# The opening of a recurrent attention kernel laid out anew: first alphas turned by quarters, unread padding left uncleared, first scores and masks chunk by chunk, the second block's k and q turned in halves

## The chip, the cores and the metric

The kernel runs on one core of one Trainium2 chip. The metric is the device time of one execution in microseconds (us), lower is better. The core has five engines that each work through an instruction list of their own: TensorE (PE, matrix multiplications, into PSUM banks), VectorE (DVE), ScalarE (ACT), GpSimd (POOL) and SyncE (SP, which here only issues DMA transfers). Engines wait for each other through semaphores.

## The reference

Two steps, one after the other, for 4 batches, 8 heads, 768 time steps, head size 48:

```python
state = zeros((B, H, D, D))
for t in range(S):                                    # gated linear attention
    state = alpha[:, :, t, :, None] * state + einsum('bhd,bhe->bhde', k[:, :, t], v[:, :, t])
    y[:, :, t] = einsum('bhd,bhde->bhe', q[:, :, t], state)
x = y.transpose(0, 2, 1, 3).reshape(B, S, H * D)      # 384 columns
val, gate = split(x @ w_in)                           # w_in 384 x 1024, halves of 512
h = exp(A_log) * h + val[:, t, :]                     # scan over t, gives ys
out = (gate * sigmoid(gate) * ys) @ w_out             # w_out 512 x 384
```

w_in and w_out arrive as 64-bit floats, of which the kernel makes 32-bit ones on the chip.

## The kernel before, in words

The work is cut into 12 blocks: 4 batches of 3 blocks of 256 steps each (N=12, NG=3, GC=256). A block has two chunks of 128 steps (c = 0, 1), a chunk two halves of 64 steps. Heads 0 to 3 lie on partitions 0 to 63 of a block's tensors and heads 4 to 7 on partitions 64 to 127; i = 0, 1 names the two groups of heads.

For each block m:

- alpha, q and k come from memory with steps on partitions (`load_steps`) in the first blocks, and are *turned* on TensorE so that head and head dimension lie on partitions: `turned` (L684) writes into a PSUM bank, `copy_turned` (L698) copies the bank into place, `turn_over`, `alphas` and `straighten` (L705 to L721) do both. A block's tensor has eight pieces j, two banks of four. For most tensors a piece is turned by two matmuls with the identity, one for each group i, each into one half of the array's columns (L694, two trace records each); for the four listed in `turned` it is a transpose of 128 columns and one of 64 (L689, L690, one record each).
- VectorE scans alpha's running product P (`scan_P`, L630) and the reverse one V (`scan_V`, L649), and multiplies Zk = k V (`scaled_k`, L614) and Zq = q P (`scaled_q`, L605).
- TensorE makes `scores` (L744), 32 trace records for each chunk; `masks` has VectorE cut the scores (L754) and ScalarE copy the K and dS parts out (L756).
- TensorE then makes the output y of values inside the block (`first_values` L862 for block 0, `values` L778 later), the block's state sums (`states`, L810), and the part carried from state sums (`first_carried` L870, `carried` L791). For block 0 `first_states` puts the sums into wide_S (ScalarE L877, VectorE L879).
- `first_join` (L884 to L887) or `join` copies y as xT, and `project(n, cc)` (L927) multiplies it by a quarter of w_in; ScalarE makes sg (L940), VectorE scans h (L932), and `output` multiplies by w_out (L956).

The weights come in six units. Each unit is converted in `convert(i)`: ScalarE makes the low part (`low`, L544, into a tile wr), VectorE two instructions of high bits (L553, L555), GpSimd adds both (L557).

Every list is written out by hand, each engine keeps the order in which the program issues its instructions, and the kernel uses eight PSUM banks: s0, s1, y0, y1 by name, and a ring of four called mm that `bank()` hands out in turn; a writer waits until the last reader of the bank's former content is done.

The opening (L982 to L1025) is a straight list. The first loads are issued on SyncE and ScalarE. The padding of several tiles is cleared by VectorE memsets (L497 to L516). After `convert(0)` a memset of one element of raw_a on GpSimd (L1001) holds back the second stream of loads: SyncE's next issue overwrites that tile, and everything SyncE issues later (alpha 2, w_in units 2 and 3, k 2, q 2, alpha 3, v 1, w_out, v 2) stands behind it. The first `project` closes the opening; block 1's scores, the turning of block 2's alpha, k and q, and project(0,1) to project(0,2) follow in the first pass of the loop:

```python
V = scan_V(1, P)
f0 = project(n, 0)
scaled_k(1, tk, V); scaled_q(1, tq, P); low(2)
f1 = project(n, 1)
convert(2); alphas(2); low(3)
first(m)                       # scores(1), masks(1)
f0(); f1()
tk = straighten(2, "k"); ...; tq = straighten(2, "q")
...
f2 = project(n, 2)
```

Of the kernel before, what the change touches and what calls it, by code (L numbers as in the profile page):

```python
# [11 lines left out]
U32 = mybir.dt.uint32  # L12
U16 = mybir.dt.uint16
AF = mybir.ActivationFunctionType
ALU = mybir.AluOpType
# [331 lines left out]
def fast(  # L347
# [27 lines left out]
    G = 2  # L375
# [117 lines left out]
    def constants():  # L493
# [18 lines left out]
        for t in dS[0] + dS[1]:  # L512
            nc.vector.memset(t[:, :, :, D:64], 0.0)
        for t in sums:
            nc.vector.memset(t[:, :, D:64], 0.0)
        nc.vector.memset(K0[:, :, :, D:], 0.0)  # L516
# [21 lines left out]

    def low(i):
        bits, w = bits_of(i)  # L540
        r = p2.tile([C, UW], I32, tag="wr", name="wr")
        lows[i] = r.rearrange("p (a n) -> p a n", a=w.shape[1])
        halves = lows[i].bitcast(U16).rearrange("p a (n two) -> p a n two", two=2)
        nc.scalar.activation(halves[:, :, :, 0], bits[:, :, :, 0], AF.Copy, scale=2.0 ** -29)  # L544

    def convert(i):
        if i not in lows:
            low(i)
        bits, w = bits_of(i)
        r = lows.pop(i)  # L550
        halves = r.bitcast(U16).rearrange("p a (n two) -> p a n two", two=2)
        quarters = bits.rearrange("p a n two -> p a (n two)").bitcast(U16).rearrange("p a (n four) -> p a n four", four=4)
        nc.vector.tensor_scalar(out=w.bitcast(U32), in0=bits[:, :, :, 1], scalar1=3, scalar2=0x3FFFFFFF,  # L553
                                op0=ALU.logical_shift_left, op1=ALU.bitwise_and)
        nc.vector.tensor_scalar(out=halves[:, :, :, 1], in0=quarters[:, :, :, 3], scalar1=0xC000, scalar2=None,  # L555
                                op0=ALU.bitwise_and)
        nc.gpsimd.tensor_tensor(out=w.bitcast(I32), in0=w.bitcast(I32), in1=r, op=ALU.add)  # L557
# [33 lines left out]
    def by_runs(t):  # L591
        return t.rearrange("p h (c j) -> p h c j", j=NJ)
# [90 lines left out]

    def turned(m, name, js, t):  # L684
        raw = steps_of(name, m)
        tp = t[:, 0:len(js) * C].rearrange("p (j x) -> p j x", j=len(js))
        if (m, name) in ((1, "k"), (1, "q"), (2, "a"), (3, "a")):
            for n, j in enumerate(js):
                nc.tensor.transpose(tp[:, n], raw[:, ds(ROW + j * D - 64, C)], ident)  # L689
                nc.tensor.transpose(tp[0:64, n], raw[:, ds(j * D, 64)], ident)  # L690
            return tp.rearrange("p j (c h) -> p h c j", h=4)
        for n, j in enumerate(js):
            for i in range(2):
                nc.tensor.matmul(tp[ds(64 * i, 64), n], raw[:, ds(i * ROW + j * D, 64)], ident,  # L694
                                 start=True, stop=True, skip_group_check=True)
        return tp.rearrange("p j (c h) -> p h c j", h=4)

    def copy_turned(to, js, tp, engine=None):  # L698
        place = by_runs(to)[:, :, :, js.start:js.stop]
        if engine:  # L700
            return engine.tensor_copy(out=place, in_=tp)
        return nc.scalar.activation(place, tp, AF.Copy)  # L702

    def turn_over(m, name, to, tags=(None, None)):
        size = NJ // len(tags)  # L705
        copies = []
        for n, tag in enumerate(tags):
            js = range(size * n, size * (n + 1))
            copy = copy_turned(to, js, turned(m, name, js, bank(tag)), nc.vector if n % 2 and tag else None)
            if tag:  # L710
                for other in copies[(n + 1) % 2::2]:
# [3 lines left out]
    def alphas(m, tags=(None, None)):  # L715
        turn_over(m, "a", by_place(als[m % 2])[:, :, 1:GP], tags)
# [31 lines left out]
    def masks(m):  # L748
        sc = [[t[:, 0:4 * (L + D)].rearrange("p (h x) -> p h x", h=4) for t in pair] for pair in scs.pop(m)]
        mb = mask[:, None, :]  # L750
        if m < NG:
            for c in range(G):
# [269 lines left out]
    first_carried((2, 3))  # L1022
    first_join()
    nc.scalar.activation(a_dec, a_log, AF.Exp)
# [196 lines left out]
```

## Time and profile before

| | us |
|---|---|
| median of 3 runs | 279.24 (279.05 to 279.8) |
| profiled execution | 279.67 |
| its span in the trace | 277.8 |
| busy: TensorE / VectorE / ScalarE / GpSimd | 271.7 / 217.8 / 110.3 / 98.2 |
| start of the first projection | 23.49 |
| SyncE's second stream of loads begins | 19.06 |

A span is the time from the first to the last instruction of the profiled execution. Rows of the chain of work that ended last give start, length, engine, output and line. Rows of an engine's timeline give start, busy time, line, operation, output<-input, shapes and count, and in brackets the idle time before with what ended it. A windows row gives, for a stretch of time, the busy time of TensorE, of its weight loads, VectorE, ScalarE and GpSimd, then the granted TensorE clock, the DMA engines' share and GB/s. "record" means one instruction of TensorE in the trace.

### The profile page before, as it was taken

The page shows a single profiled execution, that of the slowest core. Times are in us where ns is not written, and L with a number is a line of the kernel's source. Part 1 is how long each engine was busy: PE and PEld are TensorE (multiplying, and loading weights), DVE is VectorE, ACT ScalarE, POOL GpSimd, SP SyncE. Part 2 cuts the span into 40 slices and gives each one's busy share as a digit, 9 for nine tenths or more (in the row PEclk, how much of TensorE's full clock was granted, in tenths as well). Part 3 has the DMA queues.
Part 4 walks back from the last instruction along what each step waited for, and adds up shares of the span by engine and source line. Part 5 has one row for each costly group of instructions (what it writes and reads, how often), then busy time and mean ns, then how long its engine had stood idle before and what let it go on. Part 6 is the DMA issues. An engine that isn't in the chain of part 4 may idle for free.

```text
span 277.8 us, 9491 instructions
## 1 busy us (share of the span) xinstructions
PE 271.7 (98%) x4040; PEld 217.3 (78%) x4040; DVE 217.8 (78%) x281; ACT 110.3 (40%) x244; POOL 98.2 (35%) x105
## 2 busy tenths in 40 slices
PE   7999999999999999999999999999999999999995
PEld 5988987876688788788787787787787787787874
DVE  7889998898499599499499599499499598269640
ACT  2677763461325325325334334334343343341111
POOL 8131223230057155156156164164165163142000
PEclk9999999999999999999999999999999999999999
DMA  6949991935909739729659748829748711101101
GB/s 189 314 133 319 285 293 49 217 78 132 273 12 228 168 97 217 168 85 221 145 140 205 158 132 197 188 91 197 170 125 186 190 55 45 58 5 43 57 5 59
DMA packets 52462, 41.16 MB, mean 148 GB/s; under 512 B 27360, under 2 KB 50976, under 8 KB 52416
## 3 DMA queue, kind: packets, MB, share of 16 engines
q1 hardware_dynamic: 50768, 38.98, 55.3%
q10 hardware_dynamic: 1392, 0.99, 1.3%
q8 instruction: 32, 0.52, 0.8%
q0 software_dynamic: 256, 0.56, 0.7%
q14 instruction: 14, 0.11, 0.1%
HBM read 32.54 MB, written 4.72 MB: 134 GB/s over the span
## 4 chain that ended last, share of the span: by engine, by line
PE 94%; DVE 3%; DMA 1%; ACT 1%; issue 1%; SPq 0%; DVEq 0%; ACTq 0%
PE mm L927 47%; PE mm L956 20%; PE y L778 4%; PE y L791 4%; PE s L744 4%; PE mm L744 3%; PE s L810 3%; PE mm L1182 2%; DMA raw_a<-in_alpha_dram 1%; PE mm L694 1%; PE mm L689 1%; PE mm L690 1%; DVE V L649 1%; DVE P L630 1%; PE y L862 1%; PE s L694 1%
## 5 line engine op out<-in xcount | busy, mean ns | idle before, releaser
L927 PE MATMUL mm<-xT,w_in 128*128 128x256 f32 x576 | 133.4, 385 | 0.6 <-ACT xT L884 0.6
L927 PEld LDWEIGHTS mm<-xT,w_in 128*128 128x128 f32 x576 | 106.7, 190 | 17.1 <-issue 0.8
L956 PE MATMUL mm<-w_out,f_last 128*128 128x384 f32 x160 | 53.2, 486 | 0.0
L940 ACT ACTIVATE sg<-mm 128x256 f32<-128x256 f32 x48 | 18.4, 384 | 72.4 <-PE mm L927 71.9
L956 PEld LDWEIGHTS mm<-w_out,f_last 128*128 128x128 f32 x160 | 30.4, 190 | 19.1
L942 POOL TENSOR_TENSOR f_last<-sg,hh 128x256 f32<-128x256 f32 x36 | 34.3, 954 | 24.7 <-ACT sg L940 21.2
L830 POOL TENSOR_TENSOR sum<-sum,dS 128x192 f32<-128x192 f32 x30 | 31.2, 1039 | 18.2 <-ACT dS L818 16.8
L762 POOL TENSOR_TENSOR AK<-AK,mask 128x512 f32<-128x512 f32 x9 | 11.5, 1281 | 67.4 <-ACT AK L760 67.4
L649 DVE TENSOR_TENSOR_SCAN V<-al,ends 128x1028 f32<-128x1028 f32 x12 | 30.1, 2512 | 0.4
L932 DVE TENSOR_TENSOR_SCAN hh<-a_dec,hh,mm 128x256 f32<-128x256 f32 x32 | 23.1, 722 | 8.3 <-PE mm L927 8.1
L950 ACT ACTIVATE o_sb<-mm 128x384 f32<-128x384 f32 x22 | 10.8, 491 | 46.4 <-PE mm L956 46.4
L630 DVE TENSOR_TENSOR_SCAN P<-al,lower 128x1028 f32<-128x1028 f32 x12 | 27.5, 2292 | 0.4
L759 DVE TENSOR_TENSOR A<-s,mask 128x256 f32<-128x256 f32 x9 | 3.8, 425 | 29.5 <-PE s L744 29.5
L595 DVE STREAM_TRANSPOSE k<-raw_k 128x1024 f32<-128x1024 f32 x9 | 18.3, 2033 | 0.0
L595 DVE STREAM_TRANSPOSE q<-raw_q 128x1024 f32<-128x1024 f32 x9 | 18.1, 2016 | 0.0
L557 POOL TENSOR_TENSOR w_in<-w_in,wr 128x768 int32<-128x768 int32 x4 | 7.3, 1832 | 26.4 <-ACT al L702 9.5
L595 DVE STREAM_TRANSPOSE al<-raw_a 128x1024 f32<-128x1024 f32 x8 | 16.4, 2048 | 0.1
L605 DVE TENSOR_TENSOR Zq<-q,P 128x1024 f32<-128x1024 f32 (+1 forms) x14 | 15.0, 1070 | 0.3
L778 PEld LDWEIGHTS y<-AK,v 64*64 64x64 f32 x352 | 12.1, 134 | 3.6 <-issue 3.6
L614 DVE TENSOR_TENSOR Zk<-k,V 128x1024 f32<-128x1024 f32 (+1 forms) x14 | 14.7, 1050 | 0.1
L778 PE MATMUL y<-AK,v 64*64 64x64 f32 x352 | 14.5, 221 | 0.0
L778 PE MATMUL y<-A,v 64*64 64x64 f32 x352 | 14.5, 221 | 0.0
(158 smaller groups left out, 375.1 us busy)
## 6 DMA issues: line engine op xcount, KB each, us to landing
v<-in_v_dram SPq DMA_DIRECT2D x22, 192.0 KB, 4.0
out_dram<-o_sb SPq DMA_DIRECT2D x22, 192.0 KB, 4.2
raw_k<-in_k_dram SPq DMA_DIRECT2D x18, 184.0 KB, 3.6
raw_q<-in_q_dram SPq DMA_DIRECT2D x18, 184.0 KB, 4.2
raw_k<-in_k_dram SPq DMA_DIRECT2D x18, 176.0 KB, 4.1
raw_q<-in_q_dram SPq DMA_DIRECT2D x18, 176.0 KB, 4.3
raw_a<-in_alpha_dram SPq DMA_DIRECT2D x16, 184.0 KB, 5.2
raw_a<-in_alpha_dram SPq DMA_DIRECT2D x16, 176.0 KB, 5.1
```

The costliest lines, as they stand in the source:

```text
L595: nc.vector.transpose(out=by_runs(to).rearrange("p h c j -> p h j c"), in_=raws[name][:, 0:4 * ROW].rearrange("p (h j d) -> p h j d", h=4, ...
L605: nc.vector.tensor_mul(Zqs[m % 2][:, ds(u0, n), :, D:].rearrange("p u h t -> p h u t"), t[:, :, at].rearrange("p h (u t) -> p h u t", t=L) ...
L630: nc.vector.tensor_tensor_scan(out=P, data0=al[:, 0:4 * GP], data1=lower.rearrange("p h t -> p (h t)"), initial=0.0, op0=ALU.mult, op1=ALU ...
L649: nc.vector.tensor_tensor_scan(out=V[:, ::-1], data0=al[:, 1:4 * GP + 1][:, ::-1], data1=ends.rearrange("p h t -> p (h t)")[:, ::-1], init ...
L744: nc.tensor.matmul(scs[m][c][i][ds(L * h, L), ds(p * (L + D), L + D)], Zk[rows, c, p, ds(h * L, L)], Zq[rows, u, p], start=True, stop=True ...
L778: nc.tensor.matmul(ys[m][i][ds(64 * s, 64), e, ds(c * C + h * L, L)], v_sb[rows, c, 4 * i + p, :], As[i][rows, c, p, :], start=across and ...
L830: nc.gpsimd.tensor_add(Ss[j][:, :, 0:D], Ss[j - 1][:, :, 0:D], part)
L927: nc.tensor.matmul((pv, pg)[vg], w_ins[cc][:, kk, vg, :], xT[:, kk, :], start=(kk == 0), stop=(kk == NK - 1))
L932: nc.vector.tensor_tensor_scan(out=hh, data0=a_dec[:, cc:cc + 1].to_broadcast([C, GC]), data1=pv, initial=prev_h[cc][:, GC - 1:GC] if n % ...
L940: nc.scalar.activation(sg, pg, AF.Silu)
L942: f = lambda: engine.tensor_mul(fs[n][cc], sg, hh)
L956: nc.tensor.matmul(os[c], fs[n][cc][:, ds(c * C, C)], w_outs[cc // 2][:, cc % 2, :], start=(cc == 0), stop=(cc == NI - 1))
```

## The change

Only the opening is edited; from `for half in range(2): load_w_out` on the program is as before.

- **Padding.** The memsets of dS, K0 (columns that no instruction reads) are dropped; those of `sums` move to GpSimd, behind the second weight conversion.
- **First alphas.** `first_alphas` turns block 0's alphas by 32 matmuls of 64x64 (a quarter of the array each) where there were 16 of 128x64, beginning with the group i = 1 of the first two pieces. The four copies, two on ScalarE and two on VectorE, each take 16 step-places of four pieces.
- **First q, k.** `first_q` turns all eight pieces of group i = 1 first and then all of i = 0, where the groups alternated. Block 0's k is turned by transposes.
- **Weights.** `convert` is cut into `room`, `low`, `high` (which can take every other row group) and `add_low`. `convert(0)` stands after the masks of block 0 and block 1's second k copy; the high bits of unit 1 are made in two parts; `low(1)` and `add_low(1)` come after `first_states`.
- **Scores, masks, second block.** Scores of block 0 are issued by chunk, masks by chunk. Block 1's k is turned in two halves, one ahead of the scores and one behind them, and its q in two halves, one behind the states and one behind the carried parts, before `first_join`.
- **Small copies.** ratio and lower are copied between the scans.

The diff without its plainest lines:

```diff
@@ constants
         for t in vs:
             nc.vector.memset(t[:, :, :, D:64], 0.0)
-        for t in dS[0] + dS[1]:
-            nc.vector.memset(t[:, :, :, D:64], 0.0)
-        for t in sums:
-            nc.vector.memset(t[:, :, D:64], 0.0)
-        nc.vector.memset(K0[:, :, :, D:], 0.0)
@@ conversion
     def low(i):
+        nc.scalar.activation(room(i)[1][:, :, :, 0], bits_of(i)[0][:, :, :, 0], AF.Copy, scale=2.0 ** -29)
+
+    def high(i, part=slice(None)):
         bits, w = bits_of(i)
...
+        nc.vector.tensor_scalar(out=w.bitcast(U32)[:, part], in0=bits[:, part, :, 1], scalar1=3, scalar2=0x3FFFFFFF,
+                                op0=ALU.logical_shift_left, op1=ALU.bitwise_and)
+        nc.vector.tensor_scalar(out=halves[:, :, :, 1], in0=quarters[:, part, :, 3], scalar1=0xC000, scalar2=None,
+                                op0=ALU.bitwise_and)
+
+    def add_low(i):
+        w = bits_of(i)[1]
+        nc.gpsimd.tensor_tensor(out=w.bitcast(I32), in0=w.bitcast(I32), in1=lows.pop(i), op=ALU.add)
...
@@ turning
+    turned_by_transpose = ((0, "k"), (1, "a"), (1, "k"), (1, "q"), (2, "a"), (3, "a"))
...
-        if (m, name) in ((1, "k"), (1, "q"), (2, "a"), (3, "a")):
+        if (m, name) in turned_by_transpose:
...
+    def first_alphas():
+        raw, to = steps_of("a", 0), by_runs(by_place(als[0])[:, :, 1:GP])
+        tps = [[bank(tag)[:, 0:NJ // 2 * 64].rearrange("p (j x) -> p j x", x=64) for tag in tags]
+               for tags in (("s0", "s1"), ("y1", "y0"))]
+
+        def turn_quarter(j, i, r):
+            rows = ds(64 * r, 64)
+            nc.tensor.matmul(tps[j // 4][r][ds(64 * i, 64), j % 4], raw[rows, ds(i * ROW + j * D, 64)],
+                             ident[rows, rows], start=True, stop=True, skip_group_check=True)
+
+        for j in range(2):
+            for r in range(2):
+                turn_quarter(j, 1, r)
+        for j in range(NJ):
+            for r in range(2):
+                turn_quarter(j, 0, r)
+                if j + 2 < NJ:
+                    turn_quarter(j + 2, 1, 1 - r)
         copies = []
...
+                copy = nc.vector.tensor_copy(out=place, in_=part) if r else \
+                    nc.scalar.activation(place, part, AF.Copy)
...
+    def first_q():
+        raw, to = steps_of("q", 0), plain("q")
+        tps = [bank().rearrange("p (j x) -> p j x", x=C) for _ in range(2)]
+        for i in (1, 0):
+            for j in range(NJ):
+                nc.tensor.matmul(tps[j // 4][ds(64 * i, 64), j % 4], raw[:, ds(i * ROW + j * D, 64)], ident,
+                                 start=True, stop=True, skip_group_check=True)
...
@@ the opening's list
-    alphas(0, ("s0", "s1", "y1", "y0"))
-    tq = straighten(0, "q")
+    first_alphas()
+    tq = first_q()
     tk = straighten(0, "k")
     alphas(1)
     P = scan_P(0)
+    last = P[:, :, GC]
+    nc.scalar.activation(ratio[:, 0], last, AF.Copy, scale=1.0 / FIRST_PRODUCT)
+    nc.scalar.activation(lower[:, :, 0], last, AF.Copy)
     V = scan_V(0, P, False)
-    halves = [range(0, NJ // 2), range(NJ // 2, NJ)]
-    parts = [turned(1, "k", js, bank()) for js in halves]
+    part = turned(1, "k", halves[0], bank())
     for c in range(G):
         scaled_k(0, tk, V, c)
         scaled_q(0, tq, P, c)
-    scores(0)
     tk = plain("k")
-    for js, part in zip(halves, parts):
-        copy_turned(tk, js, part)
+    copy_turned(tk, halves[0], part)
+    for c in range(G):
+        scores(0, (c,))
+    part = turned(1, "k", halves[1], bank())
+    for c in range(G):
+        masks(0, (c,))
+    copy_turned(tk, halves[1], part)
+    high(0)
+    high(1, slice(0, None, 2))
     low(0)
-    parts = [turned(1, "q", js, bank()) for js in halves]
-    convert(0)
+    add_low(0)
     nc.gpsimd.memset(raws["a"][0:1, 0:1], 0.0)
     load_steps("a", 2, [nc.sync])
     load_w(units[2], nc.sync)
-    masks(0)
-    low(1)
     first_values(True)
     st = states(0)
-    convert(1)
+    tq = plain("q")
+    part = turned(1, "q", halves[0], bank())
     first_states(st)
-    tq = plain("q")
-    for js, part in zip(halves, parts):
-        copy_turned(tq, js, part)
-    last = P[:, :, GC]
-    nc.scalar.activation(ratio[:, 0], last, AF.Copy, scale=1.0 / FIRST_PRODUCT)
-    nc.scalar.activation(lower[:, :, 0], last, AF.Copy)
+    low(1)
+    copy_turned(tq, halves[0], part)
+    high(1, slice(1, None, 2))
+    add_low(1)
+    for t in sums:
+        nc.gpsimd.memset(t[:, :, D:64], 0.0)
...
     first_carried((1,))
     first_values(False)
     first_carried((2, 3))
+    part = turned(1, "q", halves[1], bank())
     first_join()
+    copy_turned(tq, halves[1], part)
```

More of the change, by code (lines that the diff above doesn't have):

```diff
@@ L537, in fast, with room @@
     lows = {}
+    def room(i):
+        if i not in lows:
+            r = p2.tile([C, UW], I32, tag="wr", name="wr")
+            lows[i] = r.rearrange("p (a n) -> p a n", a=bits_of(i)[1].shape[1])
+        return lows[i], lows[i].bitcast(U16).rearrange("p a (n two) -> p a n two", two=2)
     def low(i):
+        nc.scalar.activation(room(i)[1][:, :, :, 0], bits_of(i)[0][:, :, :, 0], AF.Copy, scale=2.0 ** -29)
+    def high(i, part=slice(None)):
         bits, w = bits_of(i)
[L541 to L544, printed above, removed]
+        halves = room(i)[1][:, part]
+        quarters = bits.rearrange("p a n two -> p a (n two)").bitcast(U16).rearrange("p a (n four) -> p a n four", four=4)
+        nc.vector.tensor_scalar(out=w.bitcast(U32)[:, part], in0=bits[:, part, :, 1], scalar1=3, scalar2=0x3FFFFFFF,
[5 more added lines that the diff above has]
+        nc.gpsimd.tensor_tensor(out=w.bitcast(I32), in0=w.bitcast(I32), in1=lows.pop(i), op=ALU.add)
     def convert(i):
@@ L548, in convert @@
             low(i)
[L549 to L557, printed above, removed]
+        high(i)
+        add_low(i)
     def check_w(i):
@@ L696, in turned @@
         return tp.rearrange("p j (c h) -> p h c j", h=4)
[L698 to L705, printed above, removed]
-        copies = []
[L707 to L711, printed above, removed]
+    halves = [range(0, NJ // 2), range(NJ // 2, NJ)]
@@ new lines, in copy_turned @@
+    def copy_turned(to, js, tp):
+        nc.scalar.activation(by_runs(to)[:, :, :, js.start:js.stop], tp, AF.Copy)
+    def first_alphas():
[14 more added lines that the diff above has]
+                    turn_quarter(j + 2, 1, 1 - r)
+        copies = []
+        for n in range(2):
+            for r in range(2):
+                place = to[:, :, ds(16 * r, 16), 4 * n:4 * n + 4]
+                part = tps[n][r].rearrange("p j (c h) -> p h c j", h=4)
+                copy = nc.vector.tensor_copy(out=place, in_=part) if r else \
+                    nc.scalar.activation(place, part, AF.Copy)
+                for other in copies[1 - r::2]:
@@ L718, in straighten, with turn_over, alphas @@
+    def turn_over(m, name, to):
+        for js in halves:
+            copy_turned(to, js, turned(m, name, js, bank()))
+    def alphas(m):
+        turn_over(m, "a", by_place(als[m % 2])[:, :, 1:GP])
     def straighten(m, name):
```

11 lines of the change are left out of this document (6 added, 5 removed).

## The prediction

> **What bounds the kernel now.** I read four views in turn: the page's parts 1 and 4, the chain of waits for the first 70 us, TensorE's own waits, then the timelines of the other engines up to 40 us. The page first:
>
> ```profile
> span 277.8 us, 9491 instructions
> PE 94%; DVE 3%; DMA 1%; ACT 1%; issue 1%; SPq 0%; DVEq 0%; ACTq 0%
> ```
>
> The chain that ended last is TensorE for 94% of the span, so a change pays only where it shifts TensorE's last instruction. The profiled execution took 279.67 us, 1.87 us more than its span and 0.43 us more than the 279.24 us median; I work in its microseconds and add the difference to the median.
>
> ```profile
> 4.72 1.80 PE s L694 x16
> 6.52 0.91 PE y L694 x16
> ...
> 10.59 2.31 DVE V L649
> ...
> 12.99 0.69 DVE Zk L614
> ...
> 18.53 0.90 PE y L862 x40
> ...
> 20.00 0.34 ACT wide_S L877
> ...
> 20.38 0.62 PE y L870 x22
> ...
> 22.98 0.37 ACT xT L884
> ...
> 23.49 5.42 PE mm L927 x24
> ...
> 31.58 0.77 PE mm L744 x32
> 32.35 3.64 PE mm L694 x64
> 35.99 2.79 PE mm L927 x12
> 39.40 0.72 PE s L810 x64
> PE mm L927 <- ACT xT L884: 0.6, 1, 0.6
> ```
>
> The chain's columns are start, length and work. Up to 15 us it runs over VectorE's scans P and V, then over TensorE; from the first projection (23.49) on it is TensorE almost alone, and the list of TensorE's waits between 15 and 70 us (last row) has little but the 0.6 us ahead of that projection. The change ends at that projection. So two questions decide: when it starts (23.49 now), and whether what the change delays holds up the stretch behind it, up to project(0,2) at 35.99.
>
> **The change up to the first projection.** Step by step along TensorE.
>
> First alphas. The first 16 records took 1.80 us and the next 16, of one shape, 0.91: TensorE ran at half rate until about 6.4. After, 32 quarter matmuls of 64x64 do the work, two records each, on four tiles. The nearest row is L810: 64 records of 48 columns on four tiles in 0.72, which for 64 columns gives 0.72 x 64/48 = 0.96, and at half rate 1.9. From 4.72, with a few records ahead of it because the half that arrives first goes first: an end at 6.4 (6.2 to 6.7) instead of 7.43, **1.0 us gained**. The copies are now two for each engine; those of the last bank run behind 6.4 and take 0.46 (VectorE's rows; the last is TensorE's first):
>
> ```profile
> 5.28 0.58 DVE L513 MEMSET dS<- 128x128 f32 x4
> ...
> 6.28 0.17 DVE L516 MEMSET K<- 128x128 f32 x1
> 6.56 0.46 DVE L701 COPY al<-s 128x256 f32<-128x256 f32 x1
> 1.44 2.93 PE L726 MATMUL y<-wide_S 128*128 128x256 f32 x6 [1.44 <-DVE raw_q L498]
> ```
>
> VectorE clears padding from 5.28 to 6.45 (L513 to L516: 11 memsets, the first four and the last shown) and copies at 6.56; the removal is what lets that copy run at 5.9. The six of L515 go to GpSimd at about 25, where it is idle. Behind them both scans move up 0.9: V from 10.59 to 9.7, ending at 12.0, and P ahead of it to 7.1.
>
> ```profile
> 7.21 1.93 PE L694 MATMUL mm<-ident,raw_q 128*64 128x128 f32 x32
> 8.96 1.93 PE L694 MATMUL mm<-ident,raw_k 128*64 128x128 f32 x32
> ...
> 12.56 0.33 PE L689 MATMUL mm<-ident,raw_k 128*128 128x128 f32 x1
> ...
> 14.26 0.27 PE L690 MATMUL mm<-ident,raw_k 128*64 128x128 f32 x1
> 14.46 1.00 PE L744 MATMUL s<-Zq,Zk 48*64 48x112 f32 x32
> 15.64 1.00 PE L744 MATMUL mm<-Zq,Zk 48*64 48x112 f32 x32 [0.18 <-ACT k L702]
> 10.95 0.60 ACT L702 ACTIVATE k<-mm 128x512 f32<-128x512 f32 x1 [0.30 <-PE mm L694]
> ```
>
> First q. Now two column halves alternate, 32 records start within 1.75 us (7.21 to 8.96), 0.055 each. After, eight matmuls on one half come first, then eight on the other. Bounds: 1.75 if TensorE overlaps them anyway, 3.5 if the 32 records queue singly at the 0.11 of two transposes (16 records from 12.56 to 14.37). L862 speaks for queueing: a record of its 64 columns is half of 0.11, 0.055; 40 spread evenly over four tiles would take 0.55; its order puts two thirds on one column half, whose two tiles then set 0.73; measured 0.90. I take 3.1, as the two halves overlap where they meet: **1.35 lost** (0 to 1.75). It ends at 9.6.
>
> k(0) by transposes: 16 records of 0.11, 1.75 as now, free; 11.35. a(1) then ends at 13.1. ScalarE's second copy of k ends 0.84 behind its matmuls (now 11.55 against 10.71), at 12.2, which is behind V's end (12.0), so Zk starts at 12.25 instead of 12.99. If q overlapped, V would bind at 12.1: the bad order costs the path little. Four products, 0.6 to 0.69 each, bring Zq of the second chunk to 14.8.
>
> Scores. Half of k(1) fits in 13.1 to 14.0. Scores of the chunks run from 14.1 without the wait of 0.18 on a k copy (idle ahead of 15.64), at 0.77 to 1.00 each (L744): end 15.65 to 16.1, now 16.64. The other half of k(1), 0.87, ends by 16.6; then come the first values (0.90, from 16.7 instead of 18.53) and states (0.72), done at 18.4 instead of 20.0.
>
> q(1) in halves. The first half (0.87) stands at 18.45, where TensorE now waits 0.38 for ScalarE's wide_S (20.00 to 20.38); carried parts start at 19.4 and take 2.4 to 2.6 (20.38 to 22.98 now); the second half, 21.9 to 22.8, lies over the xT copy for which TensorE now waits 0.51 (22.98 to 23.49). Each split adds two changes of shape, 0.09 each (from 14.26 to 14.46 it is 0.20 where transposes stand 0.11 apart): four make 0.36.
>
> Sum to the first projection: -1.0 +1.35 -0.18 -0.38 -0.51 +0.36 and -0.1 for the scores' pace = **-0.5**: 23.0 (22.7 to 23.5). TensorE has no gap left here; further savings elsewhere would not help.
>
> **What the change delays.** The memset of raw_a on GpSimd (L1001) stands behind convert(0), and SyncE's whole second stream of loads waits for it.
>
> ```profile
> 17.18 1.83 POOL L557 TENSOR_TENSOR w_in<-w_in,wr 128x768 int32<-128x768 int32 x1 [9.06 <-DVE AK L754]
> 18.94 0.09 POOL L1001 MEMSET raw_a<- 1x1 f32 x1
> 19.06 1.19 SPq L421 DMA_DIRECT2D raw_a<-in_alpha_dram  x2
> 28.66 1.09 ACT L544 ACTIVATE wr<-wbits 128x768 uint16<-128x768 uint32 x1 [1.23 <-DMA wbits<-in_moe_w_in_dram]
> 29.61 0.35 ACT L940 ACTIVATE sg<-mm 128x256 f32<-128x256 f32 x1
> ...
> 30.75 0.69 ACT L702 ACTIVATE al<-mm 128x512 f32<-128x512 f32 x1 [0.20 <-PE mm L690]
> ...
> 33.19 0.33 ACT L756 ACTIVATE dS<-mm 128x192 f32<-128x192 f32 x1
> 24.00:36.00 12.00, 12.00 (x168) 10.87 (x166) 11.58 (x18) 9.68 (x20) 1.84 (x1) 1.00 0.97 311
> ```
>
> Now GpSimd's add of convert(0) runs at 17.18. After, low(0), 1.09 long as at 28.66, is queued on ScalarE behind the four K and dS copies of the masks and behind the second k(1) copy (16.75 to 17.4; K and dS take 0.33 each): 17.4 to 18.5. The add takes 18.5 to 20.4, the memset follows, SyncE issues at 20.5: **1.45 later** (1.2 to 1.7). DMA is at 0.97 from 24 to 36 us, so every landing of that stream moves by about as much: wbits of unit 2, for which ScalarE waits 1.23 before 28.66, lands at 30.1. ScalarE is in order, and behind low(2) stand sg of project(0,1) (29.61 to 31.1), the alpha copies (the second 30.75 to 32.2), low(3), the K and dS copies (33.52 to 34.8). TensorE reaches the second chunk of scores(1) at 31.1, yet two of its banks come free with sg, about 31.5, so 0.4 is lost there and 0.1 to 0.4 with the masks behind it; the turning of q(2) takes the banks that the K and dS copies free, 34.8, where TensorE would arrive at 34.4, 0.4 lost, and its records, which fill 1.75, end at about 36.4. So project(0,2) starts at 36.4 against 35.99: the 0.5 won is used up and **0.4 is lost on top**. Bounds: -0.5, if these banks turn out free, and +1.45, if each landing goes through.
>
> VectorE. high(1)'s second half meets the add of convert(0), the add of convert(1) meets the scans:
>
> ```profile
> 15.41 0.55 DVE L553 TENSOR_SCALAR w_in<-wbits 128x768 uint32<-128x768 uint32 x1
> 18.19 1.26 DVE L553 TENSOR_SCALAR w_in<-wbits 128x768 uint32<-128x768 uint32 x1 [0.40 <-DMA wbits<-in_moe_w_in_dram]
> ...
> 28.53 1.22 DVE L605 TENSOR_TENSOR Zq<-q,P 128x1024 f32<-128x1024 f32 x1
> ```
>
> L553 takes 0.55 alone and 1.26 while GpSimd's add ran (17.18 to 19.01). [...] From rows alone: half of high(1), 0.3 long, may take 0.71 longer as L553 did, and V(1) between nothing and the rest of an add, some 1 us; the scans start 0.9 earlier than now, P(1) being at the head of them, so Zq(1) ends at 29.75 now and at 29.7 to 30.2 after. TensorE wants it at 30.1 (the first chunk of scores(1) runs ahead of 31.58 now, 0.93 long, less 0.5): nothing to 0.1.
>
> ```profile
> 43.76 0.55 issue
> ...
> 49.16 0.33 ACT K L756
> ```
>
> Behind 36 us the chain leaves TensorE at two places only, 0.55 without a named cause and 0.33 for a K copy, which could swallow or widen the difference; I carry 0.4 through. Profiled time 279.67 + 0.4; median 279.24 + 0.4 = **279.65**, by bounds 278.7 to 280.7. About 0.3% (0.84 us) is what a measurement of this kernel can tell from no change.
>
> **Rivals.** (1) *The stream is the new bound.* If the 1.45 goes through to q(2) and on, because raw_q(2) and the K copies both bind, project(0,2) starts 1.2 to 1.45 late: 280.4 to 280.7, slower. For it: DMA share 0.97, ScalarE in order, no slack behind low(2) but the 0.20 us in which the second alpha copy waits for TensorE. Against: banks are four, and TensorE has 3.5 us of turning that needs no weights. It decides once SyncE's first issue is past about 20.3. 0.25.
>
> (2) *The clock falls.* After, k(0), a(1) and half of k(1) make 40 transposes in a row, 9.6 to 14.0, 4.4 us; now the longest row is 16 (1.75 us, 12.56 to 14.37), behind matmuls, and the next matmuls keep full pace. If transposes alone let the clock fall for as long as the half rate lasted at the start, from the first matmul at 1.44 to 6.4, 5 us of work take twice their time from 14 us on: +2.4, 282. Against it: the 16 transposes ahead of 30.65 leave the granted clock at 1.00 (the window of 24 to 36). The trace cannot refute it for 40. 0.10. [...]
>
> (3) *Faster.* The 0.5 is kept, because sg and the copies free their banks in time, and the later pause of 0.55 goes too: 279.24 - 0.5 - 0.55 = 278.2. For it: every opening wait of TensorE (0.18, 0.38, 0.51) is covered by work. Against: the later gate. 0.23. That the change does not do as it says I set at nothing: the built order has each step where the diff puts it.
>
> **How the numbers follow.** Forecast 0.42, 279.65, so far as it ends within 0.3% either way (278.4 to 280.1); rival 1 0.25 and rival 2 0.10, slower: 0.35; rival 3 faster: 0.23. The range ends below at rival 3's centre and above 0.5 past rival 1, so that it leaves out rival 2 and half of rival 3: 278.2 to 281.2.
>
> **What would show it.** Right: alphas' last record near 6.4; P at 7.1; q's records over 3 us; 40 transposes at 0.11; states done near 18.4; project(0,0) near 23.0; SyncE's second stream at 20.5; low(2) at 30.1 behind a DMA wait; TensorE waits of some 0.4 before scores(1)'s second chunk and before q(2); project(0,2) near 36.4. Wrong: project(0,0) after 23.6 or before 22.3, a stream that starts before 19.5, a granted clock below full behind 10 us, or low(2) late with TensorE not waiting.

## The result, and the profile after

| | before | changed |
|---|---|---|
| median, 19 runs each, us | 279.55 (278.76 to 280.48) | 280.87 (279.23 to 282.7) |
| ratio of the changed to before | | 1.0042, 95% interval 1.0025 to 1.0059 |
| profiled execution / its span, us | 279.67 / 277.8 | 279.66 / 277.7 |
| the same, a second trace, us | | 281.2 / 279.5 |

The change costs 1.2 us (0.7 to 1.6), and its runs lie twice as far apart as those of before. The first profiled execution is one of its fastest, no slower than before's; the second (the first experiment) is an ordinary one. The two together show the loss. Medians are over all executions; ratios and intervals leave out three slow ones (one of experiment 5, two of experiment 6), over 1.5% above the fastest of their kernel. First the chain of the faster one, up to the first projection and behind it (start, length, work):

```profile
6.29 3.26 PE mm L742 x32
...
21.01 2.18 DVE P L633
...
23.21 1.60 DVE ratio L649
...
44.91 1.00 PE mm L781 x32
```

and the page's shares:

```profile
PE 89%; DVE 8%; issue 1%; ACT 0%; DVEq 0%
```

Before, the chain behind 23.49 was TensorE almost alone. Now it is VectorE's from 19.6 to 44.9 (the page: VectorE 8% of the chain, where it had 3%). One row stands out: the multiplication for block 1's ratio, 512 numbers, takes 1.60 us. Before, it took 0.17, and GpSimd's add of unit 1 ran ahead of the scan P(1) (21.75 there):

```profile
20.11 1.83 POOL L557 TENSOR_TENSOR w_in<-w_in,wr 128x768 int32<-128x768 int32 x1 [1.08 <-DVE wr L555]
24.14 0.17 DVE L646 TENSOR_TENSOR ratio<-P,ends 128x4 f32<-128x4 f32 x1
24.55 2.30 DVE L649 TENSOR_TENSOR_SCAN V<-al,ends 128x1028 f32<-128x1028 f32 x1
```

TensorE's rows in the faster execution:

```profile
22.94 5.35 PE L964 MATMUL mm<-xT,w_in 128*128 128x256 f32 x24
...
35.65 2.86 PE L964 MATMUL mm<-xT,w_in 128*128 128x256 f32 x12
...
45.83 2.86 PE L964 MATMUL mm<-xT,w_in 128*128 128x256 f32 x12
```

and its list of waits:

```profile
PE s L781 <- DVE Zq L608: 0.8, 2, 0.5
```

The first projection starts at 22.94 (23.49 before), project(0,2) at 35.65 (35.92), the next at 45.83 (45.98). TensorE was 0.55 us ahead, then waited 0.8 us for Zq, once ahead of scores(1) (0.28) and once in scores(2) (0.49). The first wait is lost against before; at the second place before pauses too, for 0.55 us without a named cause. At 45.83 0.15 us are left, and the span is 0.1 shorter.

Now VectorE and GpSimd around 18 to 28 us, in the faster and then in the ordinary execution:

```profile
18.01 0.43 DVE L547 TENSOR_SCALAR w_in<-wbits 128x384 uint32<-128x384 uint32 x1 [0.45 <-DMA wbits<-in_moe_w_in_dram]
18.35 0.45 DVE L549 TENSOR_SCALAR wr<-wbits 128x384 uint16<-128x384 uint16 x1
18.68 0.34 DVE L916 TENSOR_TENSOR wide_S<-s,wide_S 128x192 f32<-128x192 f32 x1
...
20.90 2.28 DVE L633 TENSOR_TENSOR_SCAN P<-al,lower 128x1028 f32<-128x1028 f32 x1
23.21 1.59 DVE L649 TENSOR_TENSOR ratio<-P,ends 128x4 f32<-128x4 f32 x1
...
25.06 2.30 DVE L652 TENSOR_TENSOR_SCAN V<-al,ends 128x1028 f32<-128x1028 f32 x1
```

```profile
18.54 1.83 POOL L554 TENSOR_TENSOR w_in<-w_in,wr 128x768 int32<-128x768 int32 x1 [10.42 <-ACT wr L541]
...
21.15 3.63 POOL L554 TENSOR_TENSOR w_in<-w_in,wr 128x768 int32<-128x768 int32 x1 [0.60 <-DVE wr L549]
```

```profile
18.61 0.43 DVE L547 TENSOR_SCALAR w_in<-wbits 128x384 uint32<-128x384 uint32 x1 [0.76 <-DMA wbits<-in_moe_w_in_dram]
18.96 2.00 DVE L549 TENSOR_SCALAR wr<-wbits 128x384 uint16<-128x384 uint16 x1
20.85 0.34 DVE L916 TENSOR_TENSOR wide_S<-s,wide_S 128x192 f32<-128x192 f32 x1
...
22.69 2.28 DVE L633 TENSOR_TENSOR_SCAN P<-al,lower 128x1028 f32<-128x1028 f32 x1
25.01 1.58 DVE L649 TENSOR_TENSOR ratio<-P,ends 128x4 f32<-128x4 f32 x1
...
26.84 2.30 DVE L652 TENSOR_TENSOR_SCAN V<-al,ends 128x1028 f32<-128x1028 f32 x1
```

```profile
18.82 1.83 POOL L554 TENSOR_TENSOR w_in<-w_in,wr 128x768 int32<-128x768 int32 x1 [10.72 <-ACT wr L541]
...
22.94 3.63 POOL L554 TENSOR_TENSOR w_in<-w_in,wr 128x768 int32<-128x768 int32 x1 [2.09 <-ACT xT L921]
```

In the faster one unit 1's weights land in time for the two instructions of the first half of high(1) to begin at 18.01 and 18.35, ahead of GpSimd's add of unit 0 (18.54): the second takes 0.45. In the ordinary one the first begins at 18.61, the add at 18.82, and the second at 18.96 takes 2.00: it waits until the add is done (20.65). Behind it in VectorE's list stand block 0's state sums (18.68 against 20.85), P(1) (20.90 against 22.69) and V(1) (25.06 against 26.84). The scans and the end (277.7 against 279.5) are 1.8 us later: 1.55 of it is the hold (2.00 less 0.45), and about 0.3 was there from the start: the first projection begins at 23.25 in the ordinary one, and VectorE's masks too are 0.3 later. The second hold is in both: GpSimd's add of unit 1 is issued under P(1) (21.15 in the faster one, 22.94 in the ordinary one), waits for the scan, runs until 24.78 or 26.57 (3.63 for what takes 1.83 alone), and the small multiplication that comes next on VectorE waits for it.

### The profile page after: what moved, and what is told of

Same layout as the page of the kernel before. It is cut to its first block, busy times and chain, and to the rows that moved or that the text cites. A ratio compares the mean times of both kernels' runs of the same rounds, so it can differ in the third digit from the quotient of the medians.

```text
span 277.7 us, 9487 instructions
## 1 busy us (share of the span) xinstructions
PE 272.3 (98%) x4040; PEld 217.8 (78%) x4040; DVE 218.2 (79%) x272; ACT 109.8 (40%) x244; POOL 100.1 (36%) x111
## 4 chain that ended last, share of the span: by engine, by line
PE 89%; DVE 8%; issue 1%; ACT 0%; DVEq 0%
PE mm L964 44%; PE mm L993 20%; PE y L815 4%; PE y L828 4%; PE s L781 3%; PE mm L781 3%; PE s L847 3%; PE mm L1227 2%; DVE P L633 2%; PE mm L694 1%; PE mm L742 1%; PE mm L695 1%; PE y L763 1%; DVE V L652 1%; DVE Zk L617 1%
## 5 line engine op out<-in xcount | busy, mean ns | idle before, releaser
L977 ACT ACTIVATE sg<-mm 128x256 f32<-128x256 f32 x48 | 18.4, 384 | 72.4 <-PE mm L964 72.0
L554 POOL TENSOR_TENSOR w_in<-w_in,wr 128x768 int32<-128x768 int32 x4 | 9.1, 2281 | 24.4 <-DVE wr L549 14.0
```

What stands on the lines that cost most here:

```text
L977: nc.scalar.activation(sg, pg, AF.Silu)
```

## The experiments

Each but the first is the changed kernel with one edit; ratios are against before, which ran beside them. Three theories: the **stream** (the prediction's: late loads hold ScalarE, and this TensorE), the **lock** (VectorE held by GpSimd's adds), and the **clock** (transposes let it fall).

**1. The changed kernel again.**

> The changed kernel itself again, for a second trace of it and as the measure for the three others. Its first profiled execution took 279.66 us, no more than before's (279.67), while the median of its runs is 1.3 us above before's: a trace of an ordinary execution is wanted. Stream theory (the second stream of loads is issued 1.5 us later, and what ScalarE does behind it holds up TensorE between 29 and 36 us): in a slower execution the wbits of unit 2 land at 30 us or later and project(0,2) starts 0.5 to 1.5 us later than 35.65. VectorE theory (ratio of block 1 waits 1.6 us for GpSimd's add, so that V(1), Zk, Zq and the scores behind them are late): TensorE waits 0.5 to 1 us for Zq(1) and again for Zq(2), with the loads where they were. [...] All: about 1.0042 of before.

280.81 us, 1.0041 (1.0023 to 1.0060). The trace is the ordinary one shown above. TensorE's waits in it:

```profile
PE s L781 <- DVE Zq L608: 0.8, 2, 0.5
PE mm L964 <- POOL w_in L554: 0.6, 1, 0.6
PE mm L694 <- DVE hh L969: 0.4, 1, 0.4
```

```profile
30.53 1.09 ACT L541 ACTIVATE wr<-wbits 128x768 uint16<-128x768 uint32 x1 [3.15 <-DMA wbits<-in_moe_w_in_dram]
```

The list names VectorE and GpSimd, not ScalarE. low(2) did come late (30.53, after waiting 3.15 for its load), as the stream theory says, but no wait in TensorE's list names it.

**2. k(0) and alpha(1) by matmuls again.**

```diff
-    turned_by_transpose = ((0, "k"), (1, "a"), (1, "k"), (1, "q"), (2, "a"), (3, "a"))
+    turned_by_transpose = ((1, "k"), (1, "q"), (2, "a"), (3, "a"))
```

> The change, but block 0's k and block 1's alphas are turned by matmuls as before instead of transposes; the row of 40 transposes becomes one of 8. Clock theory: the spread goes and 1.2 us come back, ratio 1.000 of before. Stream theory and VectorE theory: nothing moves, ratio 1.004.

280.7 us, 1.0048 (1.0031 to 1.0066): nothing came back, the clock theory falls. The traces say the same: all twelve that hold the row of 40 transposes have them 0.11 apart to the last, none at the 0.22 of half rate, with a granted clock of 1.00 (below the windows row of the change's first trace). The pace is the better sign of the two: in before's trace the granted clock reads 1.00 over the first 6 us too, where 16 records took 1.80 us and the next 16 took 0.91. Experiment 2's trace is one more of the faster kind: high(1)'s first half begins at 18.21 and 18.55, GpSimd's add at 18.73, and the span is 277.9.

```profile
6.00:14.00 8.00, 8.00 (x89) 7.56 (x78) 7.43 (x10) 4.33 (x10) 2.11 (x3) 1.00 1.05 313
```

**3. The release of the second stream ahead of the first add.**

```diff
+    nc.gpsimd.memset(raws["a"][0:1, 0:1], 0.0)
     high(0)
     high(1, slice(0, None, 2))
     low(0)
     add_low(0)
-    nc.gpsimd.memset(raws["a"][0:1, 0:1], 0.0)
```

> The change, but the memset that releases SyncE's second stream of loads stands ahead of the first weight addition on GpSimd, not behind it, so that the stream begins some 6 us or more earlier (near 12 to 15 us instead of 20.6). Stream theory: low(2) no longer waits for a load, ScalarE reaches project(0,1)'s sg at 28.5, and all of the loss comes back, ratio 0.998 to 1.000. VectorE theory: TensorE still waits for Zq(1) at 30 and Zq(2) at 44, ratio 1.002 to 1.004. Clock theory: 1.004.

281.62 us, 1.0085 (1.0050 to 1.0120): slower still, which no theory had. The release ran at 8.13 and the stream began at 11.07, right behind the first loads (20.58 in the change); the 14 us that the expectations of experiments 8 and 11 name for it is not what the trace has. A row of the chain and two windows of its trace, which is of one of the slowest executions (284.12):

```profile
19.69 3.32 issue
```

```profile
14.00:24.00 10.00, 6.68 (x230) 5.94 (x221) 7.45 (x15) 4.88 (x10) 3.24 (x2) 0.90 1.06 375
24.00:36.00 12.00, 12.00 (x136) 10.87 (x136) 9.26 (x11) 7.02 (x14) 2.80 (x8) 0.80 0.76 221
```

TensorE stands still for 3.3 us in the middle of the carried parts with nothing to wait for that the trace shows, while DMA is at 1.06; then it runs at half rate for a while: the transposes of q(1)'s second half, from 27.06 on, stand 0.21 apart, those of its first half, ahead of the pause, 0.11, and the granted clock is 0.90 over the first window and 0.80 over the second (at 0.50 that is, by estimate, from 22.0 to 28.8). What it lacked is open: one packet of an instruction queue moves at 20.5 to 21, and no run tells whether that bears on the pause. Three of the eight executions had a granted clock of 1.00 throughout and took 281.0 to 281.2, no less than the change. With such a disturbance this run does not judge the stream theory; the eighth does.

**4. The weight conversions in their old places.**

```diff
+    copy_turned(tk, halves[1], part)
+    convert(0)
+    ... the release, load_steps, load_w
     for c in range(G):
         masks(0, (c,))
-    copy_turned(tk, halves[1], part)
-    high(0); high(1, slice(0, None, 2)); low(0); add_low(0)
-    ... the release, load_steps, load_w
+    low(1)
     first_values(True)
     st = states(0)
+    convert(1)
...
-    low(1)
     copy_turned(tq, halves[0], part)
-    high(1, slice(1, None, 2)); add_low(1)
```

> The change, but the weight conversions stand where they stood before: convert(0) ahead of block 0's masks, low(1) ahead of the first values, convert(1) whole behind the states. The rest of the change stays. Stream theory: SyncE's second stream begins at 18.5 to 19.5, wbits of unit 2 land 1 us earlier, ratio 1.000. VectorE theory: convert(1)'s addition ends before the scans, ratio takes 0.2 us, V(1) ends near 26.3, TensorE finds Zq(1) ready, ratio 1.000 or 0.998; the masks are 1.2 us later, which costs TensorE some of it. Clock theory: 1.004.

280.07 us, 1.0025 (1.0004 to 1.0045): by the middles of the intervals part of it came back (the intervals overlap), but not in the way that was expected. Its list is the old one, its times (VectorE's, GpSimd's) are not:

```profile
18.82 2.18 DVE L547 TENSOR_SCALAR w_in<-wbits 128x768 uint32<-128x768 uint32 x1 [0.69 <-DMA wbits<-in_moe_w_in_dram]
...
22.59 3.04 DVE L633 TENSOR_TENSOR_SCAN P<-al,lower 128x1028 f32<-128x1028 f32 x1
```

```profile
18.74 1.83 POOL L554 TENSOR_TENSOR w_in<-w_in,wr 128x768 int32<-128x768 int32 x1 [10.64 <-ACT wr L541]
```

The add of unit 0 still starts at 18.74 (17.18 before): low(0) is behind the second k(1) copy on ScalarE, and TensorE now makes that half behind the scores. So unit 1's high bits are held for as long as in the change (2.18), where before only 0.8 us of the add were left when they came (1.26). The hold of ratio went, in exchange for one of P(1), 0.7 long (3.04 against 2.28 to 2.35). The masks, too, are later here; TensorE waits 0.5 us for them, and the first projection starts at 24.41. So the run moves more than the conversions and puts no price on them alone.

**5. All high bits of unit 1 behind the state sums.**

```diff
-    high(1, slice(0, None, 2))
...
-    high(1, slice(1, None, 2))
+    high(1)
```

> The change, but the high bits of unit 1 are all made behind block 0's state sums, where the change makes half of them ahead. Lock theory (from the traces of the change: L549 of the first half takes 0.45 us if it begins before GpSimd's add of unit 0, 2.0 us if the wbits land 0.5 us later and the add is first, and everything on VectorE up to 45 us moves by 1.8 us with it): the state sums are never held, P(1) begins at 21.3 to 21.6 in every execution (20.9 and 22.7 in the two traces of the change), the slow executions go: median 279.9 to 280.3, a spread of 1 us. Stream theory: nothing moves, ratio 1.004.

280.46 us, 1.0051 (1.0026 to 1.0075). P(1) begins at 21.23, just ahead of the 21.3 to 21.6 expected. Five of its eight runs lie within 0.5 us (280.1 to 280.6), but the others took 281.1, 282.9 and 284.3, so the spread of 1 us that was expected is not shown, nor a time clear of the change's. (A load that landed 2 us late disturbs its trace behind 29 us, so its later times are not compared.) Most of the first hold is avoided, 0.4 us of it remains (0.97 for L547, which takes 0.55 alone), and the second stays whole:

```profile
19.83 0.97 DVE L547 TENSOR_SCALAR w_in<-wbits 128x768 uint32<-128x768 uint32 x1
...
21.23 2.28 DVE L633 TENSOR_TENSOR_SCAN P<-al,lower 128x1028 f32<-128x1028 f32 x1
23.54 1.60 DVE L649 TENSOR_TENSOR ratio<-P,ends 128x4 f32<-128x4 f32 x1
```

A miss in size: of the 0.6 to 1 us expected (280.87 to 279.9 or 280.3) 0.4 came back by the medians, nothing by the ratio (1.0051 against 1.0042). V(1) still begins at 25.40, 0.34 behind the faster trace of the change (25.06), since high(1) whole stands ahead of P(1) now.

**6, 7. One add left out.** In each, GpSimd adds 8 of the 768 columns of one unit:

```diff
     def add_low(i):
-        w = bits_of(i)[1]
-        nc.gpsimd.tensor_tensor(out=w.bitcast(I32), in0=w.bitcast(I32), in1=lows.pop(i), op=ALU.add)
+        w, r = bits_of(i)[1], lows.pop(i)
+        if i == 1:                                   # i == 0 in the other
+            w, r = w[:, 0:1, 0:8], r[:, 0:1, 0:8]
+        nc.gpsimd.tensor_tensor(out=w.bitcast(I32), in0=w.bitcast(I32), in1=r, op=ALU.add)
```

> The change, but GpSimd adds the low bits of unit 1 for 8 columns only (the rest of that addition is left out). Lock theory: the multiplication for ratio (block 1) no longer waits for the add, 0.2 instead of 1.6 us, V(1) begins 1.4 us earlier, TensorE's waits for Zq (0.8 us) and for the add ahead of project(0,1) (0.6 us in the slower trace) go: ratio 1.000 to 1.002 of before, still with two groups of executions. Stream theory: 1.004.

279.9 us, 1.0016 (0.9992 to 1.0041).

> The change, but GpSimd adds the low bits of unit 0 for 8 columns only (the rest is left out); the release of the second stream behind it comes at 18.7 instead of 20.5. Lock theory: no instruction of high(1) is held, P(1) begins at 20.3 to 20.8 whenever the wbits land, all executions are like the fastest of the change or better: ratio 0.998 to 1.000. Stream theory: the same, since its stream is back at the time of before: this run alone does not tell the two apart, the one with the release on VectorE does.

279.61 us, 1.0006 (0.9991 to 1.0020). In the first, ratio is back to 0.17 while the hold by unit 0's add is there; in the second it is the other way round:

```profile
17.99 2.03 DVE L549 TENSOR_SCALAR wr<-wbits 128x384 uint16<-128x384 uint16 x1
...
24.08 0.17 DVE L651 TENSOR_TENSOR ratio<-P,ends 128x4 f32<-128x4 f32 x1
```

```profile
18.48 0.43 DVE L549 TENSOR_SCALAR wr<-wbits 128x384 uint16<-128x384 uint16 x1
...
22.96 1.59 DVE L651 TENSOR_TENSOR ratio<-P,ends 128x4 f32<-128x4 f32 x1
```

Against the change (1.0042) the add of unit 1 is worth 0.7 us and that of unit 0 1.0 us, by the middles of the intervals, times 279.6. The first ratio lies in the range expected (1.000 to 1.002), the second just above its own (0.998 to 1.000); the interval of the first allows all between nothing and 1.4. In the second the stream, released behind the shortened add, also begins earlier (18.49), so this run alone does not tell the lock from the stream.

**8. The release of the stream on VectorE, 3 us earlier.**

```diff
     high(0)
+    nc.vector.memset(raws["a"][0:1, 0:1], 0.0)
     high(1, slice(0, None, 2))
     low(0)
     add_low(0)
-    nc.gpsimd.memset(raws["a"][0:1, 0:1], 0.0)
```

> The change, but the memset that releases the second stream of loads is on VectorE behind the high bits of unit 0, so that the stream begins at 17.6 to 18 instead of 20.6, and nothing else moves. Stream theory: low(2) finds its load by 27.5, ratio 1.000 or below. Lock theory: VectorE and GpSimd go as in the change, ratio 1.003 to 1.005; a little more if the early stream delays something, as when it began at 14 (there TensorE stood still for 3.3 us).

280.61 us, 1.0031 (1.0013 to 1.0050). The stream begins at 17.51, earlier than before's 19.06, and the time stays with the change's:

```profile
17.51 1.19 SPq L421 DMA_DIRECT2D raw_a<-in_alpha_dram  x2
```

```profile
27.70 1.08 ACT L541 ACTIVATE wr<-wbits 128x768 uint16<-128x768 uint32 x1 [0.42 <-DMA wbits<-in_moe_w_in_dram]
```

```profile
19.23 1.27 DVE L547 TENSOR_SCALAR w_in<-wbits 128x384 uint32<-128x384 uint32 x1 [1.82 <-DMA wbits<-in_moe_w_in_dram]
...
22.58 2.29 DVE L633 TENSOR_TENSOR_SCAN P<-al,lower 128x1028 f32<-128x1028 f32 x1
```

```profile
37.34 2.86 PE L964 MATMUL mm<-xT,w_in 128*128 128x256 f32 x12
```

By the middles of the intervals 0.3 us came back (1.0042 less 1.0031), and the intervals overlap for the most part. The traces say more: low(2) runs at 27.70, 2.8 us earlier than in the ordinary trace of the change, and project(0,2) begins at 37.34 against 37.44 there, with a span of 279.4 against 279.5. VectorE was held as there (P(1) at 22.58 against 22.69), though at another instruction: the weights landed later here, and it is the first of the two, at 19.23, that waits for the add. So low(2) came 2.8 us earlier and TensorE, which waited for Zq as before, did not: the stream theory falls as the cause of the loss.

**9. Both adds in thirds**, with the release of the stream behind the second third of unit 0.

```diff
+        for n in range(3 if i < 2 else 1):
+            at = ds(2 * n, 2) if i < 2 else slice(None)
+            nc.gpsimd.tensor_tensor(out=w[:, at].bitcast(I32), in0=w[:, at].bitcast(I32), in1=r[:, at], op=ALU.add)
```

> The change, but GpSimd adds the low bits of units 0 and 1 in three pieces each (256 of 768 columns, by the two lengths measured, 1.83 us for 768 and 0.20 for 8, some 0.74 us a piece), so that VectorE can be held by one piece at a time; the release of the second stream stands behind the second piece, near 20.2. Lock theory: high(1)'s first half is held 0.7 us at the most instead of 1.8, ratio of block 1 0.7 instead of 1.6, P(1) at 21 to 21.6, ratio 1.000 to 1.002 of before, no group of executions 1.8 us apart. If the hold is not by the instruction: as the change, 1.004.

280.47 us, 1.0029 (1.0012 to 1.0047). The hold is by instruction, as the lock theory says, but the 1.000 to 1.002 that was expected is missed; the gain is partly lost again:

```profile
23.92 0.51 DVE L653 TENSOR_TENSOR ratio<-P,ends 128x4 f32<-128x4 f32 x1
```

```profile
21.86 5.91 POOL L556 TENSOR_TENSOR w_in<-w_in,wr 128x256 int32<-128x256 int32 x3 [1.56 <-DVE wr L549]
```

```profile
PE mm L968 <- DVE lower L647: 1.3, 1, 1.3
```

ratio takes 0.51. But now GpSimd's pieces wait in their turn behind the scans P(1) and V(1): three of them take from 21.86 to 27.77, and TensorE waits 1.3 us for them ahead of project(0,1). (The list names VectorE's small copy at 27.17 that ended with the last piece.)

**10, 11. Block 2's alphas ahead of project(0,1)**, on top of the thirds, the second of them with the release on VectorE behind high(1)'s first half:

```diff
             f0 = project(n, 0)
+            alphas(2)
             scaled_k(1, tk, V)
             scaled_q(1, tq, P)
-            low(2)
             f1 = project(n, 1)
             convert(2)
-            alphas(2)
             low(3)
```

> The one before with block 2's alphas turned ahead of project(0,1), and unit 2's low bits behind that projection, so that neither the late add of unit 1 nor the late load of unit 2 stands in front of TensorE. Lock theory with the opening's gain of 0.55 us at the first projection kept: 278.8 to 279.4, ratio 0.998, better than both kernels. If project(0,1) at its new place holds scores(1) up instead: 1.000 to 1.002.

280.89 us, 1.0040 (1.0019 to 1.0061).

> The second of this set with the release of the second stream on VectorE behind the first half of unit 1's high bits, near 18.9 instead of 20.2. Lock theory: as the second, 278.8 to 279.4, and fewer executions far above their median, since the load of unit 2 has 1.3 us more. If the earlier stream disturbs what TensorE is doing at 20 us (it stood still for 3.3 us when the stream began at 14): slower than the second by more than 0.5.

280.93 us, 1.0039 (1.0018 to 1.0061). Both expectations miss by about 1.5 us, and the earlier release did not bring fewer late executions: three of twelve lie above 282, none in experiment 10. The wait of project(0,1) moved to its bank, which VectorE's scan hh holds, and the scans are where they were:

```profile
PE mm L968 <- DVE hh L973: 0.4, 1, 0.4
```

P(1) (21.63) and V(1) (24.71) begin in experiment 10 as in experiment 9 (21.60, 24.68). So the 0.6 to 0.9 us that TensorE gained in its waits (1.3 there, 0.7 and 0.4 here) did not show at the end. The two traces do not start alike: the first alphas end at 6.53 in experiment 10 and at 5.84 in experiment 9, and the first projection begins at 23.64 and 22.93, so that project(0,2) begins at 36.75 and 36.83. Why the medians show no gain either stays open.

No version beat both kernels with all of the work in it.

**12. Both adds left out** (8 columns each):

> The change, but GpSimd adds the low bits of units 0 and 1 for 8 columns each only (the rest of both additions is left out). It shows what the opening is worth with nothing for VectorE to wait for. Lock theory: the sum of the two single runs, 0.9 us for the second add and 1.2 for the first, below the change: 278.6 to 279.0, ratio 0.996 to 0.998. If the two overlap (what one hold costs is hidden by the other): 279.3 to 279.6, 1.000.

278.7 us, 0.9963 (0.9948 to 0.9979), all twelve runs between 277.98 and 279.13, the narrowest of all.

```profile
23.48 0.17 DVE L651 TENSOR_TENSOR ratio<-P,ends 128x4 f32<-128x4 f32 x1
...
23.90 2.30 DVE L654 TENSOR_TENSOR_SCAN V<-al,ends 128x1028 f32<-128x1028 f32 x1
```

```profile
22.73 5.35 PE L966 MATMUL mm<-xT,w_in 128*128 128x256 f32 x24
...
35.24 2.86 PE L966 MATMUL mm<-xT,w_in 128*128 128x256 f32 x12
```

With nothing that holds VectorE, the new opening is 1.0 us faster than before, and V(1) begins at 23.90. (Before has a hold of its own, 0.71 at L553, and was not run without its adds: how much of the 1.0 us is the opening's is not shown.) From there to the change it is 2.2 us (1.0042 less 0.9963, times 279.6): the two adds, with their holds and the wait of project(0,1) for the second. The release of the stream moves with the first add, to 18.58, but that is not it: low(2) ran at 29.15, hardly before the 29.44 of the change's faster trace. Singly the adds gave 0.7 and 1.0, and both together 0.5 more than the sum; the intervals are too wide to say whether that is more than chance.

## Why the prediction was right and where it was wrong

The time lies in the stated range (278.2 to 281.2), but in the case with 0.35, slower, not in the forecast's. That the range holds it is luck: it reached so far up for rival 1, and what rival 1 describes did not happen. Step by step:

- **First alphas: 1.0 us gained, an end near 6.4.** They end at 6.29 in the faster and 6.54 in the ordinary trace. Right. Across the traces of the variants it is 5.6 to 6.5, with the moment at which the records go over to their faster pace (30 of them take 1.20 in the faster trace, 29 take 0.77 in experiment 6's, where q follows at 5.57), and since TensorE has no gap in the new opening, the first projection moves with it (0.25 and 0.3 between the two traces of the change): perhaps a part of the wider spread.
- **First q: 3.1 us.** 3.26. Right: the 32 records queue on one column half after the other (1.93 when they alternated).
- **Scans, Zk at 12.25, scores to 15.65, states near 18.4.** V ends at 11.82, Zk begins at 12.11, scores end at 15.76, states at 18.6. Right.
- **First projection at 23.0, 0.5 gained.** 22.94 and 23.25. Right.
- **SyncE's stream 1.45 later, low(2) at 30.1.** 20.58 and 20.88; 29.44 and 30.53. Right as a time, and the step after it failed: TensorE was not held there by 0.4 or 1.45. In the faster trace sg of project(0,1) ran at 30.38 and the next banks were free in time; project(0,2) started at 35.65, 0.3 before the old time, where 36.4 was forecast. Experiment 8 shows the stream 3 us earlier without effect on project(0,2). Rival 1 had the sign of the result with this mechanism, and so the wrong reason.
- **VectorE against GpSimd: "nothing to 0.1".** This is the term that was mis-sized. Experiment 12 puts it, with all that hangs on the adds, at 2.2 us. The prediction had both meetings, and took for the first the 0.71 that L553 showed before. That number was the rest of an add that had begun 1.0 us earlier; the prediction itself had moved this add to 18.5 to 20.4, over the time at which the weights land, so that the rest is up to 1.8. It also put the meeting at high(1)'s second half; in the ordinary trace the first half is held, ahead of the state sums and all that follows. For the second it let "the rest of an add, some 1 us" end in slack that its own opening had used up (Zq(1) wanted at 30.1): it was needed in full.
- **V(1): "between nothing and the rest of an add, some 1 us".** More in both traces: the add issued under the scan P(1) waits for the scan's end (3.63 for 1.83), and the multiplication ahead of V(1) for the add's (1.59 and 1.58 for 0.17), 1.4 us.
- **Rival 2, the clock.** Refuted: 40 transposes at 0.11 in twelve traces, a granted clock of 1.00, and matmuls in their place bring nothing. No run shows the 2.4 us that it was put at. What did go with a lower clock is pauses, in the traces of experiments 3 (3.32 us) and 5 (1.95 us): the granted clock is 0.90 over 14 to 24 us in the one and 0.88 over 24 to 36 us in the other. If the lower value is 0.50, as the half rate behind the pauses suggests (transposes 0.21 apart for 0.11; 30 records of scores in 1.76, where 32 took 1.00), it fell some 2.3 us and some 1.3 us behind the last record (estimates from these means).
- **Rival 3, 278.2.** Its premise, the 0.5 kept, came true only with the adds left out: 278.7.

## What to carry to other kernels

When an edit moves an instruction that holds up those of another engine, as GpSimd's add of 1.83 us does here, price it by where it now lies against its neighbours' arrival, not by what the collision cost in the old trace: the remainder of the add cost 0.7 us before and 1.55 in the ordinary trace after, and everything queued behind the held instruction pays it. Where a list of in-order instructions hangs on a load's landing, one trace shows only one of several outcomes; take a second trace before reading a result that differs from the median. Moving work off the opening gains only as much as the next engine's slack, and here VectorE had none left.

## What the runs showed of the hardware

- A multiplication of 128x4 numbers on VectorE takes 1.59 us instead of 0.17 when a GpSimd add is running (the change; 0.17 with that add left out, experiment 6), and a GpSimd add of 1.83 us takes 3.63 when it was issued under a scan. The hold is by instruction: with the add in thirds it is 0.51.
- Which of the two goes first is decided within 0.2 us (18.35 against 18.54, 18.96 against 18.82), and is worth 1.55 us to everything behind it on VectorE.
- In the one trace of the kernel whose second stream of loads starts at 11.07 us instead of 20.58, TensorE stood still for 3.3 us without a named cause.
- The granted clock of TensorE was 0.90 over the 10 us that hold this pause and 0.80 over the next 12, with transposes 0.21 apart instead of 0.11, and 0.88 and 0.83 over the 12 us around and behind a pause of 1.95 us in experiment 5's trace; over the stretch with 40 transposes in a row it was 1.00.
